# Attention block with a gated MLP on one core: the projection lead in groups of four tiles, the first scores moved into it, and the Q/K split moved to GpSimd

## The chip, the cores and the metric

The kernel runs on one NeuronCore of a Trainium2 chip. The metric is the device time of one execution in microseconds (us). Engines are named as in the profile: PE is TensorE (PEld its weight loads), DVE VectorE, ACT ScalarE, POOL GpSimd, SP SyncE, which here only issues DMAs.

## The reference

```python
xn = layernorm(x)                                    # x: 1 x 2048 x 512, float32
qkv = (xn @ wqkv).reshape(B, S, 3, 32, 16)           # 32 heads of 16 channels
p = softmax(einsum("bhqd,bhkd->bhqk", q, k) * 16**-0.5)
s = einsum("bhqk,bhkd->bhqd", p, v).reshape(B, S, D) @ wo
h = relu(xn @ w1 + b1) ** 2                          # 512 -> 1792
g = silu(h @ w2 + b2)                                # 1792 -> 512
out = x + s * g
```

## The kernel before, in words

Products that need float32 accuracy are made of three matmuls, high x high, high x low and low x high, of operands that were split into two `float32r` parts (`terms3`). A split is a copy to `float32r` and a subtraction. `split` does both on GpSimd (or the copy on ScalarE with `hi_act`); `split_psum` copies on ScalarE and subtracts on VectorE, straight from PSUM.

The program has three stages.

**Layer norm with full-row projections.** For each of 16 row tiles, `ln_stats`, `ln_norm`, `ln_high` and `ln_low` normalise, transpose on TensorE and split into `xT`. Between them `pump` issues projection matmuls over all 128 array rows, 12 to a tile (`q_tile`): V tiles, and tiles 0 and 4 of Q and K (`m` = 0..3 is Q, 4..7 is K, `c` the block of 512 rows). `q_end` evacuates a finished tile. A V tile is copied to `vt` and stored to `v_d`. A Q or K tile is split into `hl` (3 buffers) and stored to `q_d` or `k_d`, from which `load_k` and `load_q_pair` later read the layouts `ka`, `qm` and `qe`.

**The lead.** The other projection tiles run as two halves of 64 contraction rows each (`lead_halves`), because two 64-row matmuls in different halves of the array run side by side. Both halves of one tile add into the same PSUM bank, so the second half may start only after the first is done: it carries a dependency on a later instruction of the first half's row group (`follow`). The lower half of tile b runs next to the upper half of an earlier tile (`far`, a list 15 + `LAG` steps long). Between the projection matmuls stand the first of 2048 max matmuls (`max_mm`, 64 rows, into one of three `pm_t` banks), whose 512 columns VectorE reduces to a row maximum; the lead has five per tile. When the 64 maxima of a unit u are done, `shift(u)` turns them into two extra rows of `qe[u]`, which make the softmax shift part of the score matmul.

**The loop.** 32 units (8 groups of 4 heads, 4 blocks of 512 queries) of 16 key blocks give 512 slots `st`. Each slot has four score matmuls into `se` banks, four exponentials on ScalarE (`exp_mm`), four PV matmuls of the slot before the last (`pv_step`, `pv_mm`, into the one `po` bank), and MLP or output-projection matmuls beside max matmuls. In the last 30 slots or so, once all maxima are done, an output tile is issued in the form `wide`, with two banks and both halves at once. Which form it takes is asked when the tile begins (`m_free`).

The orders of PE, ACT, DVE and POOL are the program's own in the lead and the loop; SP is ordered by a scheduler until the loop. PSUM has three `se`, three `pm_t`, one `pd_t` and one `po` bank.

Of the kernel before, what the change touches and what calls it, by code (L numbers as in the profile page):

```python
# [8 lines left out]
F32 = mybir.dt.float32  # L9
# [7 lines left out]
P = 128  # L17
# [15 lines left out]
LAG = 8  # L33
# [3 lines left out]
EPS = 1e-5  # L37


@with_exitstack  # L40
def kernel(
# [54 lines left out]
    with ExitStack() as ph:  # L96
# [885 lines left out]
        lead = [0, 0, 0]  # L982

        def q_bank():
            lead[2] += lead[0]
            if lead[2] % 5 == 1:
                return pd.tile([P, 512], F32, name="pd_t")
            if lead[2] % 5 == 2:
                return pv.tile([P, 512], F32, name="po")
            return pe.tile([P, 512], F32, name="se")  # L990

        def q_tile(kind, m, c, last=False):
            ps = pd.tile([P, 512], F32, name="pd_t") if last else q_bank()
            for out_, lh, rh, first_, last_ in (v_terms if kind == "v" else qk_terms)(m, c, ps):
                nc.tensor.matmul(out_, lh(slice(0, P)), rh(slice(0, P)), start=first_, stop=last_)  # L995
                if not last_:
                    yield
            q_end(kind, m, c, ps, last)
            yield

        def q_end(kind, m, c, ps, last=False):
            if kind == "v":
                vt = vts[(4 * c + m) % NVT]
                nc.scalar.activation(
                    vt[:, :, :DH], ps.rearrange("p (h d) -> p h d", d=DH), AF.Copy
                )
                nc.sync.dma_start(v_d[:, c * 4 + m, :], vt.rearrange("p h d -> p (h d)"))
                lead[1] += 1
                return
            if last:  # L1010

                hl = pools["n"].tile([P, 2, 512], F32R, name="hl")
                raw = sp.tile([P, 512], F32, name="ot", bufs=1)
                nc.scalar.activation(raw, ps, AF.Copy)
                split((hl[:, 0], hl[:, 1]), raw)
                later(6, lambda: qk_store(m, c, hl))
                return
            if not lead[0]:
                hl = hlp.tile([P, 2, 512], F32R, name="hl")
                split_psum(hl[:, 0], hl[:, 1], ps)  # L1020
            else:
                hl = hlp.tile([P, 2, 512], F32R, name="hl")
                raw = hlp.tile([P, 512], F32, name="raw", bufs=2)
                nc.scalar.activation(raw, ps, AF.Copy)
                split((hl[:, 0], hl[:, 1]), raw)
            qk_store(m, c, hl)
# [9 lines left out]
        def lead_halves(kind, m, c):  # L1036
            ps = q_bank()
            mms = (v_terms if kind == "v" else qk_terms)(m, c, ps)
            done = [None]

            def emit(mm, lane, follow):
                r = slice(64 * lane, 64 * lane + 64)
                out_, lh, rh, first_, last_ = mm
                inst = nc.tensor.matmul(  # L1044
                    out_, lh(r), rh(r),
                    start=first_ and lane == 0, stop=last_ and lane == 1,
                    skip_group_check=True,
                )
                if follow:
                    tc.add_manual_dep(  # L1050
                        inst.ins, done[0].ins.name,
                        mybir.DependencyInfo(
                            mybir.DependencyClass.Sync, mybir.DependencyReason.DATA
                        ),
                        reason="the other row tile is done with the bank",
                    )
                if lane and last_:
                    q_end(kind, m, c, ps)

            def behind(inst):  # L1060
                done[0] = inst

            return [
                [lambda mm=mm, lane=lane: emit(mm, lane, lane and mm is mms[0]) for mm in mms]
                for lane in range(2)
            ], behind
# [88 lines left out]
        for i in range(NT + 3):  # L1155
# [26 lines left out]
            if i == 11:  # L1182
                raw_r = [load_w("wv", 3 * P, ((P, 3 * P),))]
            if i >= 5:
# [15 lines left out]
        for n in range(8):  # L1200
            load_k(0, n)
        qms[0] = load_q(0, "qm")
# [3 lines left out]
        for n in (2, 3):  # L1206
            fill_ring("ka", n, 1.0)
        rest += [
            ("qk", m, c) + ((True,) if (m, c) == (7, 3) else ())
            for c in range(4) for m in (1, 5, 2, 6, 3, 7)  # L1210
        ]
        pump(48, 1)
        if not isinstance(rest[0], tuple):
            for _ in rest.pop(0):
                pass
        warm = const.tile([P, 1], F32, name="warm")
        nc.scalar.activation(warm, eps_t, AF.Exp)
        lead[0] = 1
        after_v = None
        b = 0  # L1220
        far = [None] * (15 + LAG)

        def step(near):
            for mine in near:
                if mine is not None:
                    mine()
                if far and far[0] is not None:
                    far[0]()
                del far[:1]

        while len(rest) > 1:
            now[0] = b - 100
            shift_due()
            (low, high), behind = lead_halves(*rest.pop(0))
            low[6:6] = [lambda: max_mm(0)] * (1 + b % 2)
            low.append(lambda behind=behind: behind(max_mm(0)))
            high[4:4] = [lambda: max_mm(1)]
            high[9:9] = [lambda: max_mm(1)]
            if b % 2 == 0:
                high.append(lambda: max_mm(1))  # L1240
            if b < 2:
                for i in range(len(far)):
                    if far[i] is None and i % 5 == 2:
                        far[i] = lambda: max_mm(1)
            far += high
            step(low)
            max_end()
            if b == 1:
                raw_r = [load_w("wv", 3 * P, ((D + P, 3 * P),))]
            if b == 5:  # L1250
                for ko in range(KO):
                    split_w(wr_t, ko, slice(3 * P, 6 * P), raw_r[0][:, ko])
                ln.close()
                pools["v"] = ph.enter_context(tc.tile_pool(name="vp", bufs=1))
            if b in (4, 5, 8, 9):
                load_q_pair(b // 8, "qe", b % 2, qes.setdefault(b // 8, []))
            if after_v is None and lead[1] == NT:
                after_v = b
            if after_v is not None:
                k = b - after_v  # L1260
                if k == 2:
                    s1.close()
                    ep = ph.enter_context(tc.tile_pool(name="ep", bufs=1))
                    free_pt.extend(ep.tile([P, 512], F32, name=f"pt{i}") for i in range(NPT))
                    pools["n"] = ph.enter_context(tc.tile_pool(name="np", bufs=1))
                if k == 4:
                    load_v(0)
                    nc.sync.dma_start(
                        b1_t, b1.rearrange("(fo p) -> p fo", p=P), allow_slow_non_contiguous=True
                    )  # L1270
                    nc.sync.dma_start(b2_t, b2[None, :].to_broadcast([P, D]))
                if 1 <= k < 9:
                    load_k(1, k - 1)
            if b % 2 and b < 16:
                c, i = divmod(b // 2, 2)
                nc.sync.dma_start(
                    xn_d[i, :, :, c * 512 : (c + 1) * 512], xTs[c][:, i].bitcast(F32)
                )
            b += 1
        while far:  # L1280
            step([lambda: max_mm(0)] + [None] * 2)
        max_end()
        m0[0] = sum(done_m)
        assert (1, 1) in kas and "n" in pools and 0 in vs, (b, after_v)
        first.close()
# [3 lines left out]
        def exp_mm(st, j, pts, spare):  # L1289
# [6 lines left out]
            if spare and "w" in free_ps:  # L1296
# [11 lines left out]
            return nc.scalar.activation(pts[j], se, AF.Exp, scale=0.25)  # L1308

# [26 lines left out]
        pts = {}  # L1336

        def slot(st, mms, post, fill=0):
# [19 lines left out]
            for i in range(len(other)):  # L1358
# [6 lines left out]
                if i == 1:  # L1365
                    pump(fill)
# [120 lines left out]
        for st_ in range(NU * 16):  # L1487
# [3 lines left out]
            if st_ < 2:  # L1491
                slot(st_, [], None, 6)
                shift_due()
                continue
            if st_ == 2:
                assert len(rest) == 1 and next(rest[0], None) is None
                qs.close()
            item = next(dn, None)
# [10 lines left out]
            if st_ > 1:  # L1509
                pv_step(st_ - 2, pts.pop(st_ - 2))  # L1510
# [36 lines left out]
```

## Time and profile before

| | |
|---|---|
| time, median of 3 runs | 1636.4 us (1635.16 to 1637.22) |
| the profiled execution's own time | 1634.69 us |
| its span in the trace | 1632.9 us, granted clock 0.999 |
| busy PE / PEld / DVE / ACT / POOL | 99% / 60% / 82% / 72% / 32% |
| matmul instructions, max reductions | 13615, 2048 |

The page and the trace describe one execution, whose own time is 1.8 us longer than its span. A busy PE says little here: a 512-column matmul is shown for about 390 ns, and two or more are in flight at a time, so PE reads busy also while only one half of its rows works. Numbers of matmuls in a stretch of time say more.

### The profile page before, as it was taken

How to read it: one execution, taken by the hardware profiler on the slowest of the kernel's cores; microseconds unless marked ns; L12 is line 12 of the kernel's file. 1: busy time of each engine (PE TensorE's matmuls, PEld its weight loads, DVE VectorE, ACT ScalarE, POOL GpSimd, SP SyncE). 2: the span in 40 equal slices, each digit the busy share in tenths (PEclk: the TensorE clock that was granted, in tenths of full speed). 3: DMA queues.
4: the chain of work that ended last, by engine and by line, in shares of the span. 5: the costliest groups of instructions: out<-in, count | busy, mean ns of one | idle time of the engine just before them, and what ended most of it. 6: DMA issues, size and time to landing. Idle time of an engine off the chain costs nothing.

```text
span 1632.9 us, 35365 instructions
## 1 busy us (share of the span) xinstructions
PE 1614.9 (99%) x13615; PEld 972.4 (60%) x13615; DVE 1343.7 (82%) x2332; ACT 1183.3 (72%) x2343; POOL 517.7 (32%) x541
## 2 busy tenths in 40 slices
PE   7999999999999999999999999999999999999998
PEld 6799566556655655565566556645665565554455
DVE  6499888888788888888888888888888888888833
ACT  6321577778777777877777778777877787777785
POOL 4446567422211321232123103211331124213334
PEclk9999999999999999999999999999999999999999
DMA  8696545335243522342334423343341442316444
GB/s 309 189 263 217 186 153 180 110 90 161 62 105 87 155 61 82 102 125 74 93 99 112 118 69 111 95 102 89 109 125 45 110 144 66 102 40 177 127 151 139
DMA packets 150464, 201.42 MB, mean 123 GB/s; under 512 B 50008, under 2 KB 67416, under 8 KB 148760
## 3 DMA queue, kind: packets, MB, share of 16 engines
q1 hardware_dynamic: 150296, 199.17, 41.9%
q8 instruction: 107, 1.75, 0.5%
q14 instruction: 61, 0.50, 0.1%
HBM read 144.84 MB, written 53.99 MB: 122 GB/s over the span
## 4 chain that ended last, share of the span: by engine, by line
PE 98%; DVE 1%; ACT 0%; DMA 0%; issue 0%; SPq 0%; DVEq 0%
PE po L376 31%; PE pm_t L303 17%; PE pd_t L237 17%; PE se L1302 16%; PE pd_t L205 6%; PE se L1044 3%; PE se L995 3%; PE pd_t L791 3%; PE pd_t L1044 1%; PE po L1044 1%; DVE mx L311 1%; PE pm_t L1302 0%; PE pm_t L1100 0%; DMA xt<-in_A_x_dram 0%; PE pd_t L995 0%; PE pm_t L825 0%
## 5 line engine op out<-in xcount | busy, mean ns | idle before, releaser
L311 DVE TENSOR_REDUCE mx<-pm_t 128x1 f32<-128x512 f32 x2048 | 1267.7, 683 | 205.2 <-PE pm_t L303 125.7
L1308 ACT ACTIVATE pt<-se 128x512 f32<-128x512 f32 x1741 | 926.3, 616 | 230.1 <-PE se L1302 156.0
L303 PE MATMUL pm_t<-ka,qm 64*128 64x512 f32 x2048 | 785.7, 417 | 2.3 <-DVE mx L311 1.0
L1302 PE MATMUL se<-qe,ka 64*128 64x512 f32 x2009 | 730.5, 411 | 0.0
L376 PE MATMUL po<-pt,v 128*32 128x512 f32 x3560 | 527.7, 603 | 0.0
L303 PEld LDWEIGHTS pm_t<-ka,qm 64*128 64x128 f32 x2048 | 359.5, 184 | 221.8 <-DVE mx L311 201.8
L1302 PEld LDWEIGHTS se<-qe,ka 64*128 64x128 f32 x2009 | 349.8, 184 | 97.3 <-ACT pt L1308 61.2
L237 PEld LDWEIGHTS pd_t<-xc,w1s 64*128 64x128 f32 x2352 | 295.2, 187 | 51.3 <-issue 49.5
L237 PE MATMUL pd_t<-xc,w1s 64*128 64x256 f32 x2352 | 323.0, 286 | 0.0
L237 PE MATMUL pd_t<-w2t,hT 64*128 64x512 f32 x936 | 253.8, 406 | 0.0
L376 PE MATMUL po<-ex,v 128*32 128x512 f32 x536 | 223.9, 602 | 0.0
L237 PEld LDWEIGHTS pd_t<-w2t,hT 64*128 64x128 f32 x936 | 159.1, 184 | 48.9 <-issue 41.1
L1308 ACT ACTIVATE ex<-se 128x512 f32<-128x512 f32 x268 | 163.2, 620 | 34.2 <-PE se L1302 16.5
L376 PEld LDWEIGHTS po<-pt,v 128*32 128x32 f32 x3560 | 87.8, 108 | 155.4 <-issue 140.5
L555 POOL TENSOR_TENSOR r<-r 128x512 f32<-128x512 f32 x49 | 50.9, 1040 | 331.1 <-ACT r L552 331.1
L574 POOL TENSOR_TENSOR u<-u,b_t 128x512 f32<-128x512 f32 x16 | 20.6, 1286 | 354.7 <-ACT u L573 354.7
L205 PE MATMUL pd_t<-w2t,hT 64*128 64x512 f32 x408 | 106.0, 392 | 0.0
L205 PEld LDWEIGHTS pd_t<-w2t,hT 64*128 64x128 f32 x408 | 72.5, 184 | 9.7 <-DVE mx L311 0.6
L414 POOL TENSOR_TENSOR ot<-ot,hl 128x512 f32<-128x512 f32 x31 | 39.9, 1286 | 119.8 <-DMA hl<-r_d 74.7
L791 PE MATMUL pd_t<-wot,oc 64*128 64x512 f32 x267 | 76.1, 404 | 0.0
L1044 PE MATMUL se<-xT,wr_t 64*128 64x512 f32 x360 | 74.6, 391 | 0.0
L81 POOL TENSOR_TENSOR hT<-r,hT 128x512 fp32r<-128x512 f32 x56 | 72.3, 1290 | 4.7
(132 smaller groups left out, 1182.7 us busy)
## 6 DMA issues: line engine op xcount, KB each, us to landing
w1s<-w_d SPq DMA_DIRECT2D x196, 256.0 KB
xn_d<-xT SPq DMA_DIRECT2D x8, 1024.0 KB
k_d<-hl SPq DMA_DIRECT2D x32, 256.0 KB
q_d<-hl SPq DMA_DIRECT2D x16, 512.0 KB
qm<-q_d SPq DMA_DIRECT2D x128, 64.0 KB
qe<-q_d SPq DMA_DIRECT2D x128, 64.0 KB
ka<-k_d SPq DMA_DIRECT2D x32, 256.0 KB
hl<-r_d SPq DMA_DIRECT2D x31, 256.0 KB
```

The costliest lines, as they stand in the source:

```text
L81: (lo or nc.gpsimd).tensor_tensor(dst[1], raw, dst[0].bitcast(F32), op=ALU.subtract)
L205: mm = nc.tensor.matmul(out_, lh(r), rh(r), start=first_ and lane == 0, stop=last_ and lane == 1, skip_group_check=True,)
L237: mm = nc.tensor.matmul(out_, lh(r), rh(r), start=first_ and lane == 0, stop=last_ and lane == 1, skip_group_check=True,)
L303: nc.tensor.matmul(ps, qms[u][p][64 * j : 64 * j + 64, qb * P : (qb + 1) * P], kas[qd, p][64 * j : 64 * j + 64, kc * 512 : (kc + 1) * 512] ...
L311: return nc.vector.tensor_reduce(mxs[u][:, c, kc : kc + 1], ps, axis=AX.X, op=ALU.max)
L376: nc.tensor.matmul(po[32 * j : 32 * j + 32, :], vs[qd][:, (4 * kb + j) * VW : (4 * kb + j) * VW + 32], pts[j], start=(kb == 0), stop=(kb = ...
L555: nc.gpsimd.tensor_tensor(r, r, r, op=ALU.mult)
L791: inst = nc.tensor.matmul(ps[lane], oc[r, a, n, ts_], wot[r, b, n], start=m == 0 and (lane == 0 or wide), stop=m == kos and (lane == 1 or ...
L995: nc.tensor.matmul(out_, lh(slice(0, P)), rh(slice(0, P)), start=first_, stop=last_)
L1044: inst = nc.tensor.matmul(out_, lh(r), rh(r), start=first_ and lane == 0, stop=last_ and lane == 1, skip_group_check=True,)
L1302: nc.tensor.matmul(se, kas[qd, j // 2][b : b + 64, kb * P : (kb + 1) * P], qes[u][j // 2][b : b + 64, :], start=True, stop=True,)
L1308: return nc.scalar.activation(pts[j], se, AF.Exp, scale=0.25)
```

## The change

The lead has no lag list any more. It runs eight groups of four tiles (`lead_group`). In a group, row half 0 (lane 0) does its half of tiles 0 and 2 and then of tiles 1 and 3; lane 1 does tiles 1 and 3 first and then 0 and 2. So both lanes always have a projection matmul, 48 each, and 11 max matmuls each at places that `LEAD_AT` lists (after so many projection matmuls; in the first group only from the twelfth on). What was done at each tile of the old loop is now `event(b)`, called every 12 matmuls of lane 0. One full-row tile fewer runs ahead of the lead, and the full-row tile that stood in slots 0 and 1 of the loop is part of the last group, so that the lead has 32 tiles where it had 30.

The last group also issues the eight scores and exponentials of slots 0 and 1, all through one `se` bank. The loop starts at slot 2. The last two tiles of the lead stay in their `pd_t` and `po` banks; `held_ends` copies them out at the start of slot 2, and GpSimd splits them in slot 3.

In the layer-norm stage Q and K tiles of blocks 0 to 2 are copied to `raw` by ScalarE and split by GpSimd; only block 3 keeps `split_psum`. In the lead, tiles 2 and 6 of block 3 have their high part copied by ScalarE. The loads of `ka` and `qm` for the first unit are issued in turn, two memsets of `ka` move to events 2 and 3, and the loads of `b1` and `b2` move ahead of the lead.

```diff
-LAG = 8
+LEAD_AT = (
+    (3, 8, 12, 17, 22, 26, 31, 36, 40, 45, 48),
...
@@ q_end
-            if last:
...
-            if not lead[0]:
-                hl = hlp.tile([P, 2, 512], F32R, name="hl")
+            hl = hlp.tile([P, 2, 512], F32R, name="hl")
+            if not lead[0] and c == 3:
                 split_psum(hl[:, 0], hl[:, 1], ps)
             else:
-                hl = hlp.tile([P, 2, 512], F32R, name="hl")
                 raw = hlp.tile([P, 512], F32, name="raw", bufs=2)
                 nc.scalar.activation(raw, ps, AF.Copy)
-                split((hl[:, 0], hl[:, 1]), raw)
+                split((hl[:, 0], hl[:, 1]), raw, hi_act=c == 3 and m in (2, 6))
@@ lead_halves
-                if lane and last_:
-                    q_end(kind, m, c, ps)
+                if lane != lane0 and last_:
+                    if hold:
+                        held.append((m, c, ps))
+                    else:
+                        q_end(kind, m, c, ps)
...
-        pump(48, 1)
+        pump(36, 1)
...
+        def lead_group(g):
+            items = [rest.pop(0) for _ in range(4)]
+            pools_ = [(pe, "se"), (pe, "se"), (pd, "pd_t"), (pv, "po")]
...
+            last = g == groups - 1
+            se = pe.tile([P, 512], F32, name="se") if last else None
+            streams = []
+            for lane in range(2):
+                own, other = parts[lane::2], parts[1 - lane :: 2]
+                mms = own[0][0] + own[1][0] + other[0][1] + other[1][1]
+                at = [i for i in LEAD_AT[lane] if g or i >= 12]
+                signs = [own[0][2], own[1][2]]
+                ops = []
+                for i, mm in enumerate(mms):
+                    if lane == 0 and i % 12 == 0:
+                        ops.append(lambda b=4 * g + i // 12, mm=mm: [event(b), mm()])
+                    else:
+                        ops.append(mm)
+                    if i + 1 in at:
...
+                        ops.append(m)
+                    if last and i % 12 == (2, 8)[lane]:
+                        kb, j = divmod(2 * (i // 12) + lane, 4)
+                        ops.append(
+                            lambda kb=kb, j=j: exp_mm(kb, j, pts.setdefault(kb, {}), False, se)
+                        )
...
+            for pair in zip(*streams):
+                for op in pair:
+                    op()
...
+        def held_ends():
+            tp = tl.enter_context(tc.tile_pool(name="tl", bufs=2))
+            for m, c, ps in held:
+                hl = tp.tile([P, 2, 512], F32R, name="thl")
+                raw = hl[:, 1].bitcast(F32)
+                nc.scalar.activation(raw, ps, AF.Copy)
+                later(1, lambda hl=hl, raw=raw: split((hl[:, 0], hl[:, 1]), raw))
+                later(3, lambda m=m, c=c, hl=hl: qk_store(m, c, hl))
+
+        for st_ in range(2, NU * 16):
...
-            if st_ < 2:
-                slot(st_, [], None, 6)
...
+            if st_ == 2:
+                held_ends()
```

What the change does to the order is seen best at three places. On VectorE, in the layer-norm stage (`xT` is the low part of a normalised tile, `hl` the low part of a K tile) there stands before:

```order
L1108 TENSOR_TENSOR xT1_188<-pm_t_420,xT1_188 128x4x128
L87 TENSOR_TENSOR hl_458<-se_427,hl_458 128x512
L1080 BN_STATS stats_468<-xt_230 128x6
L1082 BN_AGGR mv_470<-stats_468 128x2
L1089 RECIPROCAL rstd_440<-rstd_440 128x1
```

and now:

```order
L1097 TENSOR_TENSOR xT1_188<-pm_t_420,xT1_188 128x4x128
L1069 BN_STATS stats_470<-xt_230 128x6
L1071 BN_AGGR mv_472<-stats_470 128x2
L1078 RECIPROCAL rstd_440<-rstd_440 128x1
L1079 TENSOR_SCALAR rstd_440<-mv_438,rstd_440 128x1
```

The subtraction for the K tile is gone from VectorE's row; it stands on GpSimd as a pair of operations between the memsets of the stage.

On TensorE, at the start of the lead, the last full-row tile (128 rows, line L995 before, L991 now) is followed before by one lane with its first max matmul after three projection matmuls:

```order
L995 MATMUL se_834<-wa_t_185,xT2_189 128x512 x12
L995 MATMUL se_849<-wa_t_185,xT2_189 128x512 x12
L1044 MATMUL pd_t_866<-wa_t_185,xT2_189 128x512 x3
L303 MATMUL pm_t_871<-ka0_202,qm0_199 128x512
L1044 MATMUL pd_t_866<-wa_t_185,xT2_189 128x512 x3
```

and now (the first two and the last of 24 projection matmuls that alternate between two banks, then the first max matmul):

```order
L991 MATMUL se_832<-wa_t_185,xT2_189 128x512 x12
L1030 MATMUL se_859<-wa_t_185,xT2_189 128x512
L1030 MATMUL se_860<-wa_t_185,xT2_189 128x512
...
L306 MATMUL pm_t_888<-ka0_202,qm0_199 128x512
L1030 MATMUL po_862<-wa_t_185,xT3_186 128x512
```

The first max matmul stands 24 half-row matmuls into the lead, and one full-row tile has moved behind that point.

On TensorE, at the end of the lead, `qe` marks a score. Before, the last tile's upper half runs alone with max matmuls, and the first scores come with a full-row tile (`pd_t_2416`) in slot 0:

```order
L1044 MATMUL se_2286<-xT3_186,wr_t_184 128x512 x2
L303 MATMUL pm_t_2404<-ka1_203,qm2_201 128x512
L1302 MATMUL se_2407<-qe0_747,ka0_202 128x512
L303 MATMUL pm_t_2410<-ka1_203,qm2_201 128x512
L1302 MATMUL se_2413<-qe1_748,ka1_203 128x512
L995 MATMUL pd_t_2416<-xT3_186,wr_t_184 128x512 x6
```

Now the eighth early score (into `se_2278`, the bank of all eight) stands among projection matmuls of both lanes, and what follows the lead is slot 2, with its own banks:

```order
L1230 MATMUL se_2278<-qe1_758,ka1_203 128x512
L1030 MATMUL po_2277<-xT3_186,wr_t_184 128x512
L1030 MATMUL pd_t_2276<-xT3_186,wr_t_184 128x512
...
L306 MATMUL pm_t_2533<-ka1_203,qm2_201 128x512
L1230 MATMUL se_2536<-qe0_757,ka0_202 128x512
L306 MATMUL pm_t_2539<-ka1_203,qm2_201 128x512
L1230 MATMUL se_2542<-qe1_758,ka1_203 128x512
```

From slot 2 on the two programs issue the same matmuls in nearly the same order: 177 max matmuls stood ahead of the first PV matmul before, 174 do now, and eight places of the loop have one max matmul more or fewer. Of the output tiles one now begins before the last maximum is issued and has the narrow form where it was `wide`.

210 lines of the change are left out of this document (96 added, 114 removed).

## The prediction

> **What bounds the kernel now.** I read the page first, for the chain that ended last and the busy shares, then the table of stretches for the part that the change touches, then the timelines of PE, ACT, DVE and POOL there.
>
> ```profile
> PE 1614.9 (99%) x13615; PEld 972.4 (60%) x13615; DVE 1343.7 (82%) x2332; ACT 1183.3 (72%) x2343; POOL 517.7 (32%) x541
> PE 98%; DVE 1%; ACT 0%; DMA 0%; issue 0%; SPq 0%; DVEq 0%
> ```
>
> PE is the chain. But 99% busy does not say that both row halves work; the counts of matmuls in equal stretches do.
>
> ```profile
> core 0: us, PE busy (x) PEld busy (x) DVE busy (x) ACT busy (x) POOL busy (x), PEclk, DMA share, GB/s
> 20.00:40.00 20.00, 17.27 (x88) 13.43 (x87) 13.06 (x38) 13.33 (x27) 5.21 (x6) 1.00 0.83 305
> 60.00:80.00 20.00, 19.27 (x104) 14.79 (x104) 10.34 (x17) 4.46 (x7) 11.93 (x14) 1.00 0.78 200
> 100.00:120.00 20.00, 20.00 (x176) 19.83 (x174) 18.55 (x34) 3.40 (x7) 10.99 (x14) 1.00 1.04 282
> 140.00:160.00 20.00, 20.00 (x176) 17.87 (x174) 18.37 (x31) 3.58 (x6) 11.49 (x12) 1.00 0.50 178
> 160.00:180.00 20.00, 19.65 (x137) 14.35 (x133) 19.14 (x35) 3.49 (x7) 9.54 (x10) 1.00 0.44 160
> 180.00:200.00 20.00, 18.86 (x142) 10.34 (x141) 17.11 (x29) 15.20 (x31) 12.51 (x20) 1.00 0.64 192
> ```
>
> In the middle of the lead 176 matmuls fit into 20 us, at its end 137. The steady pace comes from two evacuations ten tiles apart (ACT's timeline; the row at 119.62 is for a term below):
>
> ```profile
> 119.62 0.60 ACT L1024 ACTIVATE raw<-se 128x512 f32<-128x512 f32 x1 [2.63 <-PE se L1044]
> 123.40 0.60 ACT L1024 ACTIVATE raw<-se 128x512 f32<-128x512 f32 x1 [3.18 <-PE se L1044]
> 157.01 0.60 ACT L1024 ACTIVATE raw<-se 128x512 f32<-128x512 f32 x1 [2.89 <-PE se L1044]
> ```
>
> Ten tiles of 24 projection and 5 max half-row matmuls took 33.61 us: 33.61 / 290 = 0.1159 us for one half-row matmul when both lanes run. The stage from the last full-row tiles to the first PV matmul is bounded by these PE rows:
>
> ```profile
> 56.99 2.96 PE L995 MATMUL se<-xT,wa_t 128*128 128x512 f32 x12
> 59.78 8.56 PE L995 MATMUL se<-wa_t,xT 128*128 128x512 f32 x36
> 68.28 0.96 PE L1044 MATMUL pd_t<-wa_t,xT 64*128 64x512 f32 x3
> 69.68 0.46 PE L303 MATMUL pm_t<-ka,qm 64*128 64x512 f32 x1 [0.43 <-issue]
> 188.02 1.06 PE L376 MATMUL po<-pt,v 128*32 128x512 f32 x8
> ```
>
> The lead starts at 68.28, the first PV matmul is at 188.02: 119.74 us. In it stand 720 projection halves, 177 max and 12 score matmuls and 12 full-row matmuls, which cost two halves each: 933 halves x 0.1159 = 108.1 us. So 11.6 us of lane time are empty, by the counts above at the two ends. In the tail the wait is for VectorE:
>
> ```profile
> 163.45 4.83 DVE L311 TENSOR_REDUCE mx<-pm_t 128x1 f32<-128x512 f32 x8
> 173.63 7.86 DVE L311 TENSOR_REDUCE mx<-pm_t 128x1 f32<-128x512 f32 x13
> PEld pm_t L303 <- DVE mx L311: 6.2, 16, 0.8
> ```
>
> A queued maximum costs 4.83 / 8 or 7.86 / 13 = 0.604 us. The last row (waits from 166 to 189) shows PE's weight loads waiting 6.2 us for a free `pm_t` bank, with little else to issue.
>
> **The change, part by part.** *One full-row tile behind the start.* From 56.99 to 59.78, 12 full-row matmuls take 2.79 us; the lead starts that much earlier.
>
> *Q and K split by GpSimd in the layer-norm stage.* The subtraction on VectorE waits for a copy on ScalarE, and the next tile's statistics wait behind it:
>
> ```profile
> 28.36 0.69 DVE L87 TENSOR_TENSOR hl<-se,hl 128x512 fp32r<-128x512 f32 x1 [1.26 <-ACT hl L86]
> 29.97 0.30 ACT L1084 ACTIVATE rstd<-mv,eps_t 128x1 f32<-128x1 f32 x1 [1.64 <-DVE rstd L1089]
> 30.82 1.90 PE L995 MATMUL se<-xT,wa_t 128*128 128x512 f32 x7 [2.42 <-DVE xT L1108]
> 144.24 0.62 POOL L80 TENSOR_SCALAR hl<-raw 128x512 fp32r<-128x512 f32 x1 [1.49 <-ACT raw L1024]
> 144.94 1.30 POOL L81 TENSOR_TENSOR hl<-raw,hl 128x512 fp32r<-128x512 f32 x1
> ```
>
> VectorE sat 1.26 us and worked 0.69 us, then ScalarE sat 1.64 us, then PE 2.42 us. Without the row at 28.36 and its like before it, about 1.9 us leave this chain at each of two K or Q tiles, enough for the 2.42 us of PE. I take 2.3, between 1.2 (only one of them counts) and 2.42. The price is on GpSimd, 0.62 + 1.30 = 1.92 us a tile instead of 0.69. Four tiles are hidden in GpSimd's idle time (it works 5.21 us of the 20 from 20 to 40); uncovered, they would delay the stores to `k_d` by 1.2 us each, and only block 3's store is near the path, which stays on VectorE.
>
> [...]
>
> *The lead itself.* It has 768 projection halves, then 174 max and 12 score matmuls up to the first PV: 954 x 0.1159 = 110.6 us if both lanes are always full. To that I add four waits.
>
> (a) The first max matmul needs `ka`, loaded from what block 3's K tile stored:
>
> ```profile
> 60.01 0.43 SPq L133 DMA_DIRECT2D ka<-k_d  x1
> ```
>
> Before, it would have stood at about 68.98 (three matmuls into one lane) and ran at 69.68, 0.7 us late. Now 24 halves, 2.8 us, stand ahead of it, and the lead starts 2.79 us sooner: it would run at what was 68.28, so it waits 1.4 us, and both lanes with it. Bounds 0.7 to 2.5; one more issue ahead of it moves it.
>
> (b) VectorE. A group has 96 + 22 = 118 halves, 13.68 us, and 22 x 0.604 = 13.29 us of maxima. Only 0.39 us are left, the places at a group's border are closer than VectorE's pace, and each of the two `shift` costs more: at 119.62 the next tile came 3.78 us later instead of 3.36, 0.42 us. I take 0.2 us a group and 0.4 us a shift, 2.4 us; bounds 0.5 and 4.5.
>
> (c) Evacuation. Tiles end in pairs, and GpSimd needs 1.92 us for each, the two `raw` buffers wait for it, and it waits for `hl` buffers still being stored:
>
> ```profile
> 116.40 0.60 ACT L1024 ACTIVATE raw<-po 128x512 f32<-128x512 f32 x1 [2.88 <-POOL hl L81]
> 130.50 0.62 POOL L80 TENSOR_SCALAR hl<-raw 128x512 fp32r<-128x512 f32 x1 [3.66 <-DMA q_d<-hl]
> ```
>
> By these durations the second bank of a group's last pair is copied out some 2.2 us after its last matmul and is wanted again after 12 steps with their maxima, 3.5 us. The 1.3 us between hide the evacuation; a DMA wait like the 3.66 us row would overrun it by 2.4 us. I take 0.8 us for all groups, bounds 0 and 4.0.
>
> (d) The end. Exponentials and slots 0 to 2 before:
>
> ```profile
> 182.38 2.07 ACT L1308 ACTIVATE pt<-se 128x512 f32<-128x512 f32 x4 [1.31 <-PE se L1302]
> 182.35 2.48 DVE L311 TENSOR_REDUCE mx<-pm_t 128x1 f32<-128x512 f32 x4 [0.86 <-PE se L1302]
> ```
>
> A queued exponential costs 2.07 / 4 = 0.52 us. In the last group each early score waits for the exponential of the one before, since they share a bank. Twice ScalarE has other work in between: two evacuations at the group's start, and four copies (two `raw`, two high parts) after step 36, 4 x 0.52 = 2.1 us. Scores are some 1.4 us apart, so PE waits about 0.7 us each time. Slot 2 then has 8 halves, 0.93 us, but its four maxima need VectorE for 2.4 us and its scores wait behind the two copies of `held_ends`: another 1.6 us. Together 3.0; bounds 1.5 and 4.5.
>
> The four are 7.6 us where 11.6 were empty. First PV matmul: 68.28 - 2.79 - 2.3 + 110.6 + 7.6 = 181.4 instead of 188.0, 6.6 us earlier.
>
> *Behind it.* From there on both programs issue the same matmuls. Three maxima are done later; in the loop they fill places that stand empty, but one output tile loses the form `wide`:
>
> ```profile
> 1548.81 1.07 PE L376 MATMUL po<-pt,v 128*32 128x512 f32 x8
> 1554.48 1.06 PE L376 MATMUL po<-pt,v 128*32 128x512 f32 x8
> 1563.55 1.92 PE L376 MATMUL po<-pt,v 128*32 128x512 f32 x16
> 1567.99 1.92 PE L376 MATMUL po<-pt,v 128*32 128x512 f32 x16
> ```
>
> Two slots take 5.67 us in the narrow form and 4.44 in the wide one; a tile has four slots. Narrow visits without maxima are one or two steps shorter than this, so I take 2.0 us, between 0 and 2.5. The split of the two held tiles on GpSimd (3.8 us in slot 3) is hidden, since the MLP's first weights are split ahead of it; uncovered it would delay the third MLP tile by at most that. The early loads of `b1` and `b2` (256 KB) run beside the layer norm and I cost them at nothing, at most 1 us in (a).
>
> Sum: 6.6 - 2.0 = 4.6 us less. The profiled execution's own time is 1634.69, so 1630.1 on its scale; it lies 1.7 us under the median of 1636.4, and on the median's scale I forecast 1631.8 us.
>
> **The rivals.**
>
> *VectorE becomes the bound* (slower). If maxima cost not 0.604 but the page's mean, 0.683 us for one, a group needs 22 x 0.683 = 15.0 us instead of 13.7, and eight groups lose 10.8 us in place of the 2.4 of (b): 4.6 - 8.4, 3.8 us slower, 1640.2. It decides from 13.68 / 22 = 0.622 us on. Against it stand the two rows of 0.604 with a full queue; for it, that 22 maxima leave 3% of slack where before five per tile left 10%.
>
> ```profile
> L311 DVE TENSOR_REDUCE mx<-pm_t 128x1 f32<-128x512 f32 x2048 | 1267.7, 683 | 205.2 <-PE pm_t L303 125.7
> ```
>
> [...]
>
> *Evacuation waits for stores.* If the wait of 3.66 us falls on two or three of the eight groups, (c) is 4 to 7 us instead of 0.8, and the gain falls to about 0: 1636. For it are GpSimd's waits from 80 to 160 us before, four in the lead:
>
> ```profile
> POOL hl L80 <- DMA q_d<-hl: 7.9, 3, 3.7
> POOL hl L80 <- DMA k_d<-hl: 2.2, 1, 2.2
> ```
>
> Against it: a group's buffers have about 4 us more for their stores than the row at 130.50 had missing.
>
> *The load of `ka` does not move.* If its landing is set by the traffic (0.78 of the DMA engines in the stretch from 60 to 80) and not by the K tile, the gain of the layer norm turns into waiting at (a): 4.6 - 2.3, 1634.1.
>
> *The lead fills better.* If maxima queue without a loss and the early scores wait for nothing, the four waits are 3.5 us: 1627.7. The steady middle of the lead before, where both lanes ran without a gap, speaks for it.
>
> That the change does what it says is not in doubt: the order of instructions shows it.
>
> **How the numbers follow.** Forecast 0.55, VectorE 0.08, stores 0.14, `ka` 0.08, better filling 0.15. The likeliest gives 1631.8. The range must reach from better filling, 1627, to the stores, 1636.5; the bounds of (a) to (d) by themselves, which hardly all fall the same way, give about 4 us to each side of 1631.8, so it is 1627.0 to 1636.5. About 0.2%, 3.3 us, can be told from no change here. Faster by more than that (under 1633.1): most of the forecast's chance (0.46), all of better filling (0.15), 0.05 of the others: 0.66. Slower by more than that (over 1639.7): VectorE and a little of the stores, 0.08. Within: 0.26.
>
> **What would show it.** PE should no longer wait for `xT` near 30 us; the lead should start near 63; its tile groups should come 13.7 to 14.2 us apart, with 22 maxima in each; the first PV matmul should stand at 180 to 183, and the wait of PEld for `mx` in the tail should shrink to 1 to 3 us. The first PV matmul at 186 or later, groups over 14.5 us apart, or a later stretch of the loop that has grown by more than 2 us would prove me wrong, and the row of PE's waits there would name the cause.

## The result, and the profile after

The kernel after takes 1630.75 us (median of 8 runs, 1628.56 to 1633.15), the kernel before 1636.03 beside it (8 runs, 1634.08 to 1637.80): a ratio of 0.9966, 95% interval 0.9955 to 0.9977 (ratios here and below are of the means of the runs, not of the medians). The forecast was 1631.8, its range 1627.0 to 1636.5. The total came out; the way to it did not.

The profiled execution after takes 1631.39 us (before: 1634.69). From its page, the chain that ended last:

```profile
PE 92%; DMA 3%; issue 2%; POOL 1%; SPq 1%; ACT 0%; DVE 0%; DVEq 0%; POOLq 0%
```

PE's share of the chain fell from 98% to 92%, and DMA, issue, POOL and SPq now hold 7%. The chain now goes through transfers and through SyncE's queue, which both stood at 0% before.

The clearest view of where time came and went is the start of the same PV matmul in both traces, slot by slot. After lies ahead by 11.2 us at slot 0, by 9.2 at slot 2, by 9.4 to 8.6 from there to slot 484, by 6.8 at slot 488, by 3.7 at slot 494 and by 3.3 at the end. The rows of slot 494, before and after:

```profile
1581.31 1.92 PE L376 MATMUL po<-pt,v 128*32 128x512 f32 x16
```

```profile
1577.62 2.33 PE L379 MATMUL po<-pt,v 128*32 128x512 f32 x16
```

So 11.2 us were won before the first PV matmul, and 7.9 lost again: 7.5 at three places and 0.4 little by little in the loop.

**Before the first PV matmul.** PE's timeline after: the lead's first matmuls, the second maximum, the first PV matmul.

```profile
61.16 3.06 PE L1030 MATMUL se<-wa_t,xT 64*128 64x512 f32 x24
65.79 0.47 PE L306 MATMUL pm_t<-ka,qm 64*128 64x512 f32 x1 [0.89 <-DMA ka<-k_d]
176.83 1.07 PE L379 MATMUL po<-pt,v 128*32 128x512 f32 x8
```

The lead starts 7.12 us earlier (68.28 to 61.16). Of this, 2.79 are the 12 full-row matmuls that moved, so 4.33 come from the layer norm stage in this trace. (It is the earliest start of the seven traces with the new lead and the new split, which lie between 61.16 and 62.35.) The table of stretches, before (first two rows) and after, shows why that is more than the one labelled wait of 2.42 us:

```profile
26.00:30.00 4.00, 2.26 (x11) 1.30 (x9) 2.60 (x9) 2.05 (x5) 0.00 (x0) 1.00 0.98 363
30.00:34.00 4.00, 3.18 (x16) 2.62 (x17) 2.41 (x7) 3.16 (x6) 0.00 (x0) 1.00 0.97 357
```

```profile
26.00:30.00 4.00, 4.00 (x23) 3.31 (x22) 2.62 (x7) 2.97 (x7) 3.77 (x4) 1.00 1.00 366
30.00:34.00 4.00, 4.00 (x22) 3.25 (x21) 3.67 (x11) 2.42 (x6) 3.62 (x7) 1.00 1.01 392
```

In the second number's brackets stand PE's matmuls: 27 in these 8 us before, 45 after. The 18 that did not fit are about 3.2 us at the 45 in 8 us of after. The stretch from 14 to 18 us holds another three (21 before, 24 after), about 0.5 us. The rest of the 4.33 is not traced to a row.

The lead is then 115.67 us long instead of 119.74. At 954 halves x 0.1159 = 110.6 us, 5.1 us of it are empty. ScalarE's copies of the first pair of tiles show the cadence of the groups:

```profile
99.63 1.09 ACT L1011 ACTIVATE raw<-se 128x512 f32<-128x512 f32 x2 [9.43 <-PE se L1030]
113.46 1.09 ACT L1011 ACTIVATE raw<-se 128x512 f32<-128x512 f32 x2 [8.56 <-PE se L1030]
127.68 1.09 ACT L1011 ACTIVATE raw<-se 128x512 f32<-128x512 f32 x2 [8.96 <-PE se L1030]
141.50 1.09 ACT L1011 ACTIVATE raw<-se 128x512 f32<-128x512 f32 x2 [7.73 <-PE se L1030]
```

13.83, 14.22 and 13.82 us apart, against 13.68 for 118 halves; the group with the `shift` is the 14.22.

**Loss 1, 2.0 us at slots 2 and 3.** The first MLP matmuls wait for their operands. SP's, POOL's and PE's timelines after:

```profile
174.18 0.56 SPq L971 DMA_DIRECT2D q_d<-hl  x1
174.83 0.56 SPq L451 DMA_DIRECT2D ex<-in_B_w_dram  x1
```

```profile
180.88 0.40 POOL L83 TENSOR_SCALAR w1s<-ex 128x256 fp32r<-128x256 f32 x1 [6.73 <-DMA ex<-in_B_w_dram]
```

```profile
181.62 0.35 PE L208 MATMUL pd_t<-xc,w1s 64*128 64x256 f32 x1 [0.60 <-DMA xc<-xn_d]
...
184.39 1.07 PE L379 MATMUL po<-pt,v 128*32 128x512 f32 x8
```

From the issue of the load of the first weights (`ex`) at 174.83 to their split on GpSimd pass 6.05 us. It stands right behind a 512 KB store of a Q tile. From slot 0 to slot 2 after takes 7.56 us (176.83 to 184.39); before, where the PV matmul of slot 2 has this row, it took 5.58 from 188.02:

```profile
193.60 1.06 PE L376 MATMUL po<-pt,v 128*32 128x512 f32 x8
```

**Loss 2, 2.0 us at slots 484 to 487.** The output tile in the narrow form, PV matmuls of slots 484, 486, 488 and 490 on PE's timeline:

```profile
1550.26 1.92 PE L379 MATMUL po<-pt,v 128*32 128x512 f32 x16
1555.72 1.92 PE L379 MATMUL po<-pt,v 128*32 128x512 f32 x16
1561.18 1.92 PE L379 MATMUL po<-pt,v 128*32 128x512 f32 x16
1565.62 1.92 PE L379 MATMUL po<-pt,v 128*32 128x512 f32 x16
```

Two slots take 5.46 us in the narrow form and 4.44 in the wide one, and the tile has four slots.

**Loss 3, 3.5 us from slot 490 on.** PE waits for the last unit's `shift` rows. PE's, VectorE's and SP's timelines after:

```profile
1573.40 0.46 PE L1230 MATMUL se<-qe,ka 64*128 64x512 f32 x1 [1.43 <-DMA qe<-sh_d]
```

```profile
1562.29 0.21 DVE L347 STREAM_TRANSPOSE sq<-sh 128x32 f32<-128x32 f32 x1
```

```profile
1557.32 2.76 SPq L426 DMA_DIRECT2D on_d<-hl  x4
...
1565.25 0.38 SPq L711 DMA_DIRECT2D oc<-on_d  x1
...
1567.32 0.55 SPq L350 DMA_DIRECT2D sh_d<-sq  x1
1570.87 2.02 SPq L370 DMA_DIRECT2D qe<-sh_d  x4
```

`wo_load_last` (L711) waits until 1565.25 for the store of `on_d`, 1.6 us by SP's waits, and the store of `sq`, whose values VectorE had at 1562.50, is issued behind it and two more loads at 1567.32, 4.8 us after its values were there. Before, the same store stood ahead of `on_d`, and PE did not wait. SP's timeline before:

```profile
1565.21 0.56 SPq L347 DMA_DIRECT2D sh_d<-sq  x1
...
1573.54 3.01 SPq L423 DMA_DIRECT2D on_d<-hl  x4
```

A second price hangs on that stop. The table of stretches after, with PE's granted clock as the third number from the right:

```profile
1572.00:1573.00 1.00, 0.00 (x0) 0.00 (x0) 0.00 (x0) 0.03 (x1) 0.92 (x1) 1.00 0.03 8
...
1575.00:1576.00 1.00, 1.00 (x9) 1.00 (x7) 0.00 (x0) 1.00 (x3) 0.00 (x0) 0.54 0.79 246
1576.00:1577.00 1.00, 1.00 (x7) 0.97 (x5) 0.00 (x0) 0.95 (x2) 0.00 (x0) 0.50 0.71 262
1577.00:1578.00 1.00, 1.00 (x8) 0.20 (x8) 0.00 (x0) 0.51 (x2) 0.00 (x0) 0.50 0.00 0
1578.00:1579.00 1.00, 1.00 (x12) 0.21 (x8) 0.00 (x0) 0.57 (x2) 0.00 (x0) 0.76 0.00 0
```

A stop of 1.43 us is followed by some 3.4 us at half the clock, which cost 0.46 + 0.50 + 0.50 + 0.24 = 1.7 us: as much as the waits themselves (1.43 + 0.20).

### The profile page after: what moved, and what is told of

Its sections match the earlier page's. It is cut to its first block, busy times and chain, and to the rows that moved or that the text cites. A ratio compares the mean times of both kernels' runs of the same rounds, so it can differ in the third digit from the quotient of the medians.

```text
span 1629.6 us, 35392 instructions
## 1 busy us (share of the span) xinstructions
PE 1612.4 (99%) x13639; PEld 963.8 (59%) x13639; DVE 1341.7 (82%) x2326; ACT 1183.7 (73%) x2345; POOL 523.9 (32%) x548
## 4 chain that ended last, share of the span: by engine, by line
PE 92%; DMA 3%; issue 2%; POOL 1%; SPq 1%; ACT 0%; DVE 0%; DVEq 0%; POOLq 0%
PE po L379 29%; PE pd_t L240 17%; PE pm_t L306 16%; PE se L1230 15%; PE pd_t L208 6%; PE se L1030 3%; PE se L991 2%; PE po L1030 2%; PE pd_t L1030 1%; PE pd_t L794 1%; DMA ka<-k_d 1%; PE pm_t L1089 0%; DMA hl<-r_d 0%; DMA xc<-xn_d 0%; DMA on_d<-hl 0%
## 5 line engine op out<-in xcount | busy, mean ns | idle before, releaser
L379 PE MATMUL po<-ex,v 128*32 128x512 f32 x542 | 228.8, 603 | 0.0
L555 ACT ACTIVATE r<-pd_t,b_t 128x256 f32<-128x256 f32 x98 | 42.1, 495 | 33.0 <-PE pd_t L240 31.7
```

The source lines that it names most:

```text
L379: nc.tensor.matmul(po[32 * j : 32 * j + 32, :], vs[qd][:, (4 * kb + j) * VW : (4 * kb + j) * VW + 32], pts[j], start=(kb == 0), stop=(kb = ...
L555: nc.scalar.activation(r[:, i], ps[:, i * CW : (i + 1) * CW], AF.Relu, bias=b1_t[:, fo : fo + 1])
```

## The experiments

Theory: the split and the lead won more than forecast, and three losses, two of them not forecast, took it back. Rivals: the forecast's own sizes (2.3 us for the split, 7.6 for the four waits), and losses that belong to one profiled execution only.

**1. The split undone.**

```diff
-            if not lead[0] and c == 3:
+            if not lead[0]:
                 split_psum(hl[:, 0], hl[:, 1], ps)
```

> The kernel after, with the Q and K tiles of column groups 0 to 2 of the layer norm stage split by VectorE out of PSUM again, as before; everything else as after. Read from the two traces: the lead starts 7.12 us earlier in after, of which 2.79 are the 12 matmuls that moved and 4.33 are the layer norm stage itself. Theory (4.33 belongs to the split): the lead starts at 65.5 instead of 61.16, and the kernel takes 4.0 to 4.5 us more than after, about 1635.0. Rival A (the prediction's own term): only the one visible wait of 2.42 us comes back, so 2.3 us more, about 1633. Rival B: the later start gives the keys that the lead waits for time to land, and of the 4.33 the 1.3 us of that wait are saved: 3.0 us more.

1634.70 us (11 runs), ratio to before 0.9996 (0.9987 to 1.0005). PE's timeline:

```profile
65.58 3.05 PE L1030 MATMUL se<-wa_t,xT 64*128 64x512 f32 x24
```

The lead starts 4.42 us later than in after, and the median is 4.0 us higher: the theory holds and rival A falls. Rival B is not excluded. Its mechanism is there in a smaller size: the wait for the keys is 0.4 us instead of 0.9, the first PV matmul is 3.9 us later and the one of slot 484 only 2.9.

By the ratio, the new lead alone, with its losses, brings nothing that can be told from no change. With the losses of after the reckoning agrees: 2.79 + 4.07 (the shorter lead) = 6.9 won, 2.0 + 2.0 + 3.5 = 7.5 lost. The profiled execution of this run, 1632.44 us, is one of its two fastest: it won 7.3, lost 1.7, 2.0 and 1.6 at the three places, gained 0.3 in the loop and ended 2.3 ahead of before. Seven of the 11 runs had a mean granted clock of only 0.997 or 0.998 (three of the eight runs of after). The stop of the profiled execution at the last unit was shorter, 1.07 us, and here the clock stayed at 1.00:

```profile
1575.00:1576.00 1.00, 0.10 (x2) 0.13 (x2) 0.00 (x0) 0.00 (x0) 1.00 (x1) 1.00 0.03 8
...
1577.00:1578.00 1.00, 1.00 (x10) 1.00 (x11) 0.00 (x0) 1.00 (x3) 0.00 (x0) 1.00 0.88 299
```

Here the PV matmuls lose 1.6 us from slot 490 on, in after 3.5: the same wait has two prices, which fits the wide spread of the runs after.

**2. The split alone, on the kernel before.**

```diff
-            if not lead[0]:
+            if not lead[0] and c == 3:
                 hl = hlp.tile([P, 2, 512], F32R, name="hl")
                 split_psum(hl[:, 0], hl[:, 1], ps)
```

> The kernel before, with only the split of the Q and K tiles of column groups 0 to 2 in the layer norm stage changed to ScalarE's copy and GpSimd's split, as after has it. Theory (the split by itself is worth what the undone split cost, 4.0 us in the median): the lead starts 4.3 us earlier than in before (68.28), the wait of 2.42 us for xT is gone, and the kernel takes 3.5 to 4.3 us less than before, about 1631.5. Rival A: the gain needs the new lead, since the old one starts with the keys' load on its heels (a wait of 0.43 at its first maximum): the earlier start is given back there and 1 to 2.5 us are left. Rival B: only the visible wait, 2.3 us.

1630.25 us (four runs from 1629.52 to 1631.51, one of 1635.26), ratio 0.9966 (0.9952 to 0.9979), the ratio of the whole change. PE's first row of the lead:

```profile
64.75 0.96 PE L1044 MATMUL pd_t<-wa_t,xT 64*128 64x512 f32 x3
```

3.53 us earlier than before, and the PV matmuls stay 3.5 to 3.8 ahead to the end: rival A (given back at the keys) falls. 3.53 lies at the theory's lower edge, and rival B's 2.3 is below it. By the ratio this one edit brings as much as the whole change. By the medians it is 6.6 us (the kernel before beside it: 1636.89), more than the trace shows. The granted clock goes with that: four of these five runs had 1.000, and six of the nine runs of before had 0.998 or less. Behind the layer norm stop of 2.42 us, which is gone here, the clock stood at 0.50 in experiment 7 and at 1.00 in the trace of before (last section); that this makes the difference is not shown by a trace of before.

**3. One maximum more.** `zip` drops the last entry of the longer half in the first group, a max matmul, which is then done later, in the loop; `zip_longest` keeps it in its place. (The line that imports it is left out here.)

```diff
-            for pair in zip(*streams):
+            for pair in zip_longest(*streams):
                 for op in pair:
-                    op()
+                    if op is not None:
+                        op()
```

> The kernel after, with the one maximum restored that the pairing of the two halves drops in the first lead group (the longer half's last entry has no partner): 175 maxima before the first value matmul, not 174. By the order of the instructions this alone makes the ninth output tile use both banks again and puts the shift of the last unit ahead of the last load of the attention output. Theory: the late losses, 2.0 us at the narrow tile and up to 3.1 us at the scores of the last unit, both go; 3.5 to 5.1 us less than after, about 1626.5, and the value matmul of slot 486 is 8.8 to 9.3 us earlier than before, and so are those to the end. Rival: the loss of 3.1 us came from that one profiled execution, and only the tile's 2.0 us go: 1628.7. Rival 2: VectorE has no room for one more reduction and the lead ends 0.6 us later: 0.6 less gain in either.

1626.18 us (1625.46 to 1626.95), ratio 0.9946 (0.9932 to 0.9959): 4.6 us less than after for the place of one half-row matmul and one reduction. Against the trace of after, its PV matmuls are 0.4 later in the loop, 1.6 earlier at slot 488 (the wide form, 2.0 us), 4.7 earlier at slot 494 and 5.1 at 496. SP's timeline has the old order back, `sq` ahead of `oc`, and no row of PE's waits names `sh_d`:

```profile
1556.82 0.56 SPq L351 DMA_DIRECT2D sh_d<-sq  x1
...
1564.48 2.02 SPq L371 DMA_DIRECT2D qe<-sh_d  x4
...
1570.39 0.38 SPq L712 DMA_DIRECT2D oc<-on_d  x1
```

The theory holds. The loss was not that of one execution, and the spread of the runs falls from 4.6 to 1.5 us. Losses 2 and 3 have one root: the maxima of the loop end two slots later, and both the form of the tile and the place of the last `shift` on SP's queue follow from that.

**4. The last load put off**, the narrow tile left.

```diff
                 if k == 10:
-                    wo_load_last(1)
+                    later(4, lambda: wo_load_last(1))
```

> The kernel after, with only the last load of the attention output (its second half-kilobyte of columns, group 1) issued four slots later, so that SyncE sends the shift of the last unit first. The narrow tile stays. Theory (the order on SyncE's queue costs the 3.1 us): PE no longer waits for the last unit's shift, 2.5 to 3.1 us less than after, about 1628, and the value matmuls from slot 490 on stay 6.8 us ahead of before. Rival A: the shift itself is late (its reduction ends after the last maximum, two slots later than before), and its three transfers in a row keep PE waiting as long: 0 to 0.5 us less. Rival B: the output tile then waits for the load that was put off: no gain or up to 2 us more.

1627.49 us (1626.80 to 1628.62), ratio 0.9956 (0.9943 to 0.9968), 3.3 less than after; at slot 494 it is 3.6 us ahead of after, and the stop is gone. The theory holds, and the two losses separate: about 3.3 for the queue, the rest of experiment 3 (1.3 in the medians, 2.0 in the trace at slot 488 less what the additional maximum costs) for the form of the tile.

**5. The store behind the loads.** Q tile 2's `hl` comes from the pool that stays open, and its store goes to slot 6.

```diff
+            late_q = lead[0] and (kind, m, c) == ("qk", 2, 3)
-            hl = hlp.tile([P, 2, 512], F32R, name="hl")
+            hl = (pools["n"] if late_q else hlp).tile([P, 2, 512], F32R, name="hl")
...
+            if late_q:
+                waiting.append((6, lambda: qk_store(m, c, hl)))
+                return
             qk_store(m, c, hl)
```

> The kernel after, with the 512 KB store of the lead's last stored query tile put off to slot 6, so that the first loads of the MLP weights and of the normed rows follow on the queue without it. Theory (the loads share the DMA engines with that store): they land 1.0 to 1.5 us earlier, the first MLP matmul starts at about 180.4 instead of 181.62, and 1.0 to 1.8 us go, about 1629.3. Rival A: the loads are issued when the memory of the lead comes free (174.8, 0.3 us after its last matmul) and then take what their own 1.25 MB take; the store hardly matters: 0 to 0.4 us less. Rival B: the time between the first value matmul and the first MLP slot is set by the exponentials, and nothing changes.

1628.41 us, but from 1626.53 to 1633.21, and a ratio of 0.9964 (0.9951 to 0.9977), as after: by itself inconclusive. Its profiled execution was the slowest one. From slot 0 to slot 2 it took 6.13 us, not 7.56, but it had lost 3 us in the lead, and it lost 4.2 at the last unit, where after lost 3.5. In the lead the keys landed 1.5 us later than in after, PE stood for 1.23 us, and the clock fell to 0.50. PE's timeline and the table of stretches:

```profile
67.29 0.76 PE L306 MATMUL pm_t<-ka,qm 64*128 64x512 f32 x1 [1.23 <-DMA ka<-k_d]
```

```profile
67.00:68.00 1.00, 0.71 (x4) 0.67 (x6) 0.00 (x0) 0.00 (x0) 1.00 (x1) 0.62 0.88 189
68.00:69.00 1.00, 1.00 (x8) 0.87 (x6) 0.69 (x1) 0.00 (x0) 0.96 (x2) 0.50 0.96 266
```

**6. Both mends**, 3 and 5 together.

> The kernel of the one more maximum with the late store of the last query tile added (to slot 6): both mends, nothing else. Theory: each mend is worth what it was alone, since they lie 1,390 us apart; the store's worth, read from the stretch between the value matmuls of slots 0 and 2, was 1.43 us (7.56 to 6.13), so the median falls from 1626.2 to about 1624.8. Rival: the store's gain in the median of its own run was the luck of its executions, and the time stays at 1626.2.

1624.22 us (1623.72 to 1625.40), ratio 0.9924 (0.9911 to 0.9936); no run is as slow as the fastest of experiment 3, on the same chip. The store is worth 2.0 us in the medians and 2.1 in the traces. SP's and POOL's timelines:

```profile
174.78 0.39 SPq L452 DMA_DIRECT2D ex<-in_B_w_dram  x1
```

```profile
177.87 0.41 POOL L84 TENSOR_SCALAR w1s<-ex 128x256 fp32r<-128x256 f32 x1 [3.62 <-DMA ex<-in_B_w_dram]
```

The same load, issued at the same time, is split 3.09 us later instead of 6.05 (5.76 in the trace of experiment 3, which differs in the store alone), and slots 0 to 2 take 5.74 us. The theory holds, rival A falls. This is the best version, 6.5 us below after and 0.76% below before.

**7. Both mends without the split.** Experiment 6 with the edit of experiment 1.

> The kernel with both mends (one more maximum, late store), but with the Q and K tiles of column groups 0 to 2 of the layer norm stage split by VectorE as before: the new lead without the new split. With the split and the mends the median was 1624.2, with neither the split nor the mends 1634.7, with the split alone on the old lead 1630.3. Theory (split and lead are worth their sums: the split 4.0, the mended lead the rest): 1628.2, 0.995 of before, so that the lead that by itself brought nothing (0.9996) brings 0.45% once its two side effects are mended. Rival A: the mended gain needs the early start, because a lead that begins 4.3 us later meets the keys and the store at another time: 1630 or more. Rival B: part of the split's gain is lost in the keys' wait of the new lead, which goes without it: 1626.5 to 1627.5.

1628.81 us, ratio 0.9951 (0.9935 to 0.9968). The theory's 1628.2 holds: split and lead add up. Mended, the lead alone brings 0.49% by the ratio and 0.42% by the medians (1635.68 before; three of its eleven runs took 1639.4 to 1643.1 and raise the mean), where it brought 0.04% before the mends. The profiled execution, 1630.65 us, is the slowest of the six; behind its layer norm stop the clock fell to 0.50 (last section), and its lead started at 67.56, not at 65.58 as in experiment 1.

**8. The first maxima later**, on top of experiment 3: `i >= 17` instead of `i >= 12` in the first group, and one maximum more on each half of the second.

> The kernel of the one more maximum (the pairing mended), with the first maxima of the lead five matmuls later (from the 17th pair of the first group, not the 12th), and one maximum more on each half in the second group instead: still 175 before the first value matmul. It takes away the wait of the second maximum for the keys, 0.9 us in after and 0.2 to 1.7 in the runs since, at the price of 24 maxima in one group. Theory: TensorE's stop is gone and the lead ends 0.5 to 1.2 us earlier; the median falls from 1626.2 to about 1625.5, and the spread of the runs narrows, because the stops above 1.2 us at this place, with a granted clock of 0.67 behind them, no longer occur. Rival: VectorE is the limit of the second group, 24 x 0.625 = 15.0 us against 13.9 on TensorE, and takes 1.1 us back: no difference, 1626.2.

1626.05 us (1625.35 to 1626.49) against 1626.18: the rival holds. The wait for the keys is gone from PE's waits and nothing came of it: the lead is 115.24 us long in the trace, against 115.08 in that of experiment 3. There the wait had been 0.2 us, so that little could be won; whether the 24 maxima of the second group took something back is not shown.

**9. 24 maxima in each later group**, on top of experiment 3: positions 20 and 17 added to `LEAD_AT`.

> The kernel of the one more maximum with 24 maxima instead of 22 in each of the seven later lead groups: 189 before the first value matmul, 14 fewer in the loop. Theory (VectorE is at its limit with 22: 22 x 0.625 = 13.75 us, TensorE 118 halves x 0.1159 = 13.68): a group takes 15.0 us, not 13.8, the first value matmul is 7 to 8.5 us later than with 22, the loop gives back at most 14 x 0.116 = 1.6 us, and the kernel takes 5 to 7 us more than the one with 175, about 1632. Rival (the reductions lie beside TensorE, which has spare banks): a group takes 13.9 us, the first value matmul is 1.6 later, and the total stays at 1626.2, or falls by 2 us if one more output tile uses both banks.

1630.64 us, 4.5 more than experiment 3 by the medians and 2.6 by the ratios (0.9962 and 0.9946), for the kernel before ran slower beside this one (1636.89) than beside experiment 3 (1635.30). ScalarE's and VectorE's timeline:

```profile
116.11 1.09 ACT L1012 ACTIVATE raw<-se 128x512 f32<-128x512 f32 x2 [9.74 <-PE se L1031]
130.66 1.09 ACT L1012 ACTIVATE raw<-se 128x512 f32<-128x512 f32 x2 [9.27 <-PE se L1031]
145.18 1.09 ACT L1012 ACTIVATE raw<-se 128x512 f32<-128x512 f32 x2 [9.24 <-PE se L1031]
```

```profile
113.64 39.87 DVE L315 TENSOR_REDUCE mx<-pm_t 128x1 f32<-128x512 f32 x66
```

Groups are 14.55 and 14.52 us apart, and one queued maximum takes 39.87 / 66 = 0.604 us: 24 x 0.604 = 14.50. VectorE sets the pace (from 95 to 110 us it is busy for 14.96 of the 15 us), while PE alone would need 120 halves x 0.1159 = 13.91. The mechanism of the theory holds, its size does not: the first PV matmul is 5.7 us later counted from the lead's start, not 7 to 8.5. Up to slot 64 the trace loses more against that of experiment 3; there the clock is halved from 189.40 to 192.81 us, behind a wait of 0.76 us for `xc` (eight PV matmuls take 1.94 us at 190.76, where they took 1.06 at 184.80). From slot 64 to slot 192 the loop gives back 3.7, not 1.6; why so much is not shown. At 22 maxima in a group VectorE does not yet set the pace: in after 66 of them took 41.22 us, 0.625 each, more than the 0.604 of a full queue.

## Why the prediction was right, and where not

The total was right by luck: errors of both signs met. On the traces' scale I had 6.6 won and 2.0 lost, 4.6. The traces show 11.2 won and 7.9 lost, 3.3; the medians show 5.3. By the marks that I set myself, the working was wrong: the first PV matmul stands at 176.83, not 180 to 183, PEld's wait for `mx` in the tail (165 to 190 us) is 5.7 us, not 1 to 3, and the loop grew by far more than 2 us. The row of that wait after:

```profile
PEld pm_t L306 <- DVE mx L314: 5.7, 8, 0.8
```

What held is the absence of a wait for `xT`, and groups 13.8 to 14.2 us apart. The lead started earlier than forecast, at 61.16 and not near 63.

- *12 full-row matmuls, 2.79.* With the split undone the lead still starts 2.7 us earlier than before (68.28 to 65.58).
- *The split, 2.3.* Mis-sized: 4.33 in the trace, 4.0 in the median when undone, 3.5 in the trace of the split alone on before. The step that failed is the upper bound: I took the longest labelled wait, 2.42, for the whole hole. The count of matmuls in the stretch, 27 against 45, gives 3.2 of it. The traces show five tiles moved to GpSimd, not four. GpSimd's longer work was hidden, as costed. The subtraction takes 1.29 us on GpSimd and took 0.69 on VectorE; the move still gains 4.0 us, since VectorE's queue lay on the path and GpSimd's did not.
- *The four waits, 7.6.* They are 5.1. (a) 0.9, not 1.4; it varies from one trace to another, 0.2 us in that of experiment 3 and 1.7 in that of experiment 5. (b) 0.14 a group and 0.4 a `shift`, about 1.9, not 2.4. (c) nothing that PE waited for by name: from 61 to 177 us GpSimd waits 12.7 us for stores to `k_d` and ScalarE 3.7 us for GpSimd's `hl`, but no row of PE's or PEld's waits names `raw` or `hl`. (d) what is left of the 5.1, 2.3, not 3.0; it was not measured by itself.
- *The wide form, 2.0.* Right, to the tenth.
- *"From there on both programs issue the same matmuls."* This step hid losses 1 and 3. The matmuls are the same; their transfers are not. I followed neither the MLP's first loads past the store ahead of them, nor the last `shift` on SP's queue, which moved when the maxima ended later. I had costed those late maxima by one consequence, the form of a tile, and not by all that asks whether they are done.
- *Rivals.* VectorE as the bound has the right mechanism and point (experiment 9), but the price is 0.604 a maximum, not 0.683, so that 22 still fit. Stores held up the evacuation, but not as far as PE. The keys' load did move: the gain of the split arrived. The lead did fill better, though not to 3.5 us.

Settled in part: why the runs before spread over 3.7 us. Of the 16 runs of before beside experiments 1, 3, 4 and 5, the twelve with a mean granted clock of 0.999 took 1634.14 to 1636.00 us and the four with 0.998 took 1636.17 to 1637.23. One stretch of 3.4 us at half the clock is 0.001 of such a run and costs 1.7 us. It is not the whole spread: beside experiment 2 one run at 0.999 took 1637.85.

## What to carry to other kernels

Where an engine stands still, size the hole by the work that a stretch holds with and without it, not by the longest wait with a name. When a step moves, list everything that asks "is it done yet": here one max matmul out of 2048, moved from the first lead group into the loop, changed the form of a tile and the order on a queue some 1,480 us later, and cost 4.6 us. At the seam of two stages, let the loads that the next stage starts with go ahead of stores that nobody waits for (2.0 us here, experiment 6).

## What the runs showed of the hardware

- Some stops of PE were followed by a granted clock of 0.50 for 3.4 us, others were not, and the length of the stop does not decide it alone. After 1.43 us (after, rows from 1575 on, above), 1.23 us (experiment 5, rows from 67 on), 2.40 us (experiment 5, last unit) and 0.76 us (experiment 9) it was 0.50; after 1.07 us (experiment 1, last unit) and 0.89 us (after, the keys) it stayed at 1.00. The stop of 2.42 us in the layer norm stage left it at 1.00 in before:

```profile
29.00:30.00 1.00, 0.00 (x0) 0.00 (x0) 0.93 (x5) 0.03 (x1) 0.00 (x0) 1.00 0.86 324
30.00:31.00 1.00, 0.18 (x1) 0.18 (x2) 1.00 (x3) 1.00 (x3) 0.00 (x0) 1.00 0.80 293
```

  The same stop in experiment 7 was followed by half the clock (PE's timeline and the table of stretches):

```profile
31.65 3.18 PE L992 MATMUL se<-xT,wa_t 128*128 128x512 f32 x7 [2.42 <-DVE xT L1102]
```

```profile
31.00:32.00 1.00, 0.35 (x1) 0.35 (x2) 1.00 (x3) 1.00 (x3) 0.00 (x0) 0.55 1.05 408
32.00:33.00 1.00, 1.00 (x3) 0.81 (x3) 0.93 (x5) 0.82 (x3) 0.00 (x0) 0.50 1.05 408
```

  What decides between the two is not shown.
- A 256 KB load right behind a 512 KB store was used 6.05 us after its issue (5.76 in experiment 3), and 3.09 us after it without that store (experiment 6), issued at the same moment.
- A maximum over 128x512 from PSUM takes 0.604 us when VectorE's queue is full: 39.87 us for 66 of them at 24 a group (experiment 9), 7.86 us for 13 in before.
